# Preparing operands beside a matmul stream: a ring of seven buffers, sums in one engine's order, six steps a pair, and weight preparation spread over steps

## The chip, the cores and the metric

One core of a Trainium2 chip. The metric is the time of one execution on the device in microseconds (us), lower is better. TensorE (PE) multiplies; VectorE (DVE), ScalarE (ACT) and GpSimd (POOL) do the elementwise work; every DMA is issued from SyncE's queue (SP), one after the other.

## What is computed

An attention with packed queries, then two MLPs over its 4608 tokens, cut from the reference:

```python
p_packed = sm_attn(p, k, v)            # 8 batches, 8 heads, 576 tokens, 32 packed queries
x = sm_attn(q, p_packed, p_packed)     # -> 4608 tokens x 512
h = np.maximum(x @ moe_w_in, 0.0)      # first MLP, 2048 wide, squared relu
y = h * h @ moe_w_out
h = y @ moe2_w_in                      # second MLP, 1024 wide
solu = h * softmax(h)
out = (layernorm(solu) * g_ln) @ moe2_w_out
```

All tensors are float32. A product in full precision is made of three fast passes: each operand is split into a rounded part `hi` and a rest `lo`, and `hi*hi + hi*lo + lo*hi` is summed in PSUM. A split costs a cast on ACT (`hi`) and a subtraction on DVE or POOL (`lo`).

## The kernel before

**The stream of steps.** After the first attention stage the kernel runs 256 steps in program order, one per (batch, half of its 576 tokens, chunk of 128 of the 2048 columns), 32 steps per batch. Step i counts from `T0`, so `clock[0]` is `T0 + i`. In a step, `h1` makes six matmuls of 288 columns from a `slot` (attention output folded with `w_in`, loaded from the scratch tensor `pw_d`), ACT takes the relu, POOL squares it (line 420, `gg`; in the first twenty steps ACT does), ACT squares it again as the rounded part (line 421), DVE subtracts (the `split_lo` on line 422, whose instruction is on line 56), and three steps later `ymm` adds twelve matmuls into four PSUM tiles `Y`. After 16 steps `Y` is copied out by ACT and DVE (lines 445 and 447) and the result `y` goes to the scratch tensor `y_d`.

**Side work on the same steps.** `at_step(i, fn)` hangs a job on step i. `load_slot(b, s)` stands 13 steps ahead of the step that reads the slot; for batch 4 the slots wait for the last products `pw`, and slot 7 of it is loaded in step 138 and read in step 142. Three things run in steps 129 to 230:

- `pre_y(m)` (line 690) turns 256 tokens of `y` into the seven operands of a Strassen product for the second MLP, for 14 pairs m. It loads `yf` (one buffer) in its first step i0; `operands` then makes four sums (`comb`, line 668) and seven splits (`split`, casts on line 675, subtractions on line 676), in the steps i0+2 to i0+6; each operand lies in a `yo` tile from a ring of five and is stored to `yc_d` three steps after it was made. The first pair starts at step `R0` = 129 and the next one every `RD` = 7 steps.
- `wi_unit` and `wx_unit` decode the weights of the second MLP, one piece every five steps from step 138 on (`Decode`: a load `raw`, one ACT and three DVE instructions). The last piece of a group calls `quads` (line 585): seven casts on ACT (line 591), seven subtractions (line 592) and four sums (line 587) on DVE, all in one step; its seven stores to `wi_d` or `wx_d` are issued in the step after. There are two such groups for `w_in2` and four for `w_out2`.
- The attention jobs of batches 5 to 7 and the slots' loads.

**What sets the order.** All DMAs are pinned to program order on SP: one that has to wait holds up all that are behind it. The casts of `pre_y`, its sums and subtractions, and the casts of `quads` are pinned too; the rest is placed in each engine's queue by a planner at build time, and each queue runs in that order. After step 230 the pools of the side work are closed, and the weights and first operands of the second MLP are fetched (`load_wi`, `fetch_y`); `h2(0)`, its first product, stands in step 249.

Of the kernel before, what the change touches and what calls it, by code (L numbers as in the profile page):

```python
# [12 lines left out]
F32R = mybir.dt.float32r  # L13
# [9 lines left out]
P = 128  # L23
# [9 lines left out]
def f(ap):  # L33
    return ap.bitcast(F32)


def build(tc, qT, kT, vP, pT, w_in, w_out, w_in2, w_out2, g_ln, out):
# [3 lines left out]
    V, A, G, PE, SP = nc.vector, nc.scalar, nc.gpsimd, nc.tensor, nc.sync  # L41


    pin = tc.keep_in_program_order

    def mm(*a, **k):
        pin(PE.matmul(*a, **k))  # L47
# [4 lines left out]
    def dma(out, in_):  # L52
        pin(SP.dma_start(out=out, in_=in_))

    def split_lo(eng, lo, x, hi):
        eng.tensor_tensor(out=lo, in0=x, in1=f(hi), op=ALU.subtract)  # L56
# [16 lines left out]
    def bank(name):  # L73
        return ps.tile([P, 512], F32, tag="a", name=name, bufs=4)
# [26 lines left out]
    def t25(k, name, dt=F32):  # L101
        return mp.tile([P, KC * P], dt, tag="e" + k, name=name, bufs=2 if k == "1" else 4)
# [157 lines left out]
    T0 = 10  # L260
    ring, clock = [0], [0]
# [141 lines left out]
    def h1(n):  # L403
        b, half, fc = n
        c = slice(half * HF, (half + 1) * HF)
        pb = bank("h1")
        w = slot[b, fc // 2][:, :, fc % 2]
        i = 0
        for g in range(2):
            ah, al = at[b, g]  # L410
            for l, x in ((0, ah), (1, ah), (0, al)):
                mm(pb[:, :HF], w[:, g, l], x[:, c], start=(i == 0), stop=(i == 5))
                i += 1
        rg, g2 = t25("1", "rg"), t25("2", "ghl", F32R)
        r, gg, gh, gl = rg[:, :HF], rg[:, HF:S], g2[:, :HF], g2[:, HF:S]
        A.activation(r, pb[:, :HF], AF.Relu)  # L416
        if clock[0] < T0 + 20:
            A.activation(gg, r, AF.Square)
        else:
            G.tensor_tensor(out=gg, in0=r, in1=r, op=ALU.mult)  # L420
        A.activation(gh, r, AF.Square)  # L421
        split_lo(V, gl, gg, gh)
        gt[n] = (gh, gl)
# [44 lines left out]
    def at_step(i, fn):  # L468
        jobs.setdefault(i if i == "first" else T0 + i, []).append(fn)
# [30 lines left out]
    for b in range(2, B):  # L500
        base = (b - 1) * 32
        js = [s2_jobs(b, g) for g in range(2)]
# [3 lines left out]
        js = [j for x in zip(*js) for j in x]  # L506
# [25 lines left out]
    W2 = {}  # L532
# [30 lines left out]
    def wi_unit(k, q):  # L563
        r0, c0 = (k + 2 * (q // 2)) * P, (q % 2) * 1024

        def fin(wf):
            wq[q] = wf[:, 0]
            if q == 3:
                quads(wi_d[k], 512, *(wq[i] for i in range(4)))

        return Decode(W2["d"], w_in2[r0:r0 + P, c0:c0 + 1024], (1, 512), fin, bufs=(3, 1, 6))

    def wx_unit(k, half):
        q = k + 4 * half

        def fin(wf):
            A.activation(wf[:, 0], wf[:, 0], AF.Copy, scale=W2["g"][:, q:q + 1])
            for i in range(2):
                wq[2 * half + i] = wf[:, 0, i * 256:(i + 1) * 256]
            if half:  # L580
                quads(wx_d[k], 256, *(wq[i] for i in range(4)))

        return Decode(W2["d"], w_out2[q * P:(q + 1) * P], (1, 512), fin, bufs=(3, 1, 6))

    def quads(dst, n, b11, b12, b21, b22):
        def sub(out, x, y):
            V.tensor_tensor(out=out, in0=x, in1=y, op=ALU.subtract)

        def split(o, x):
            t = W2["d"].tile([P, 1024], F32R, tag="op", name="op", bufs=5)  # L590
            pin(A.copy(t[:, :n], x))
            V.tensor_tensor(out=t[:, n:2 * n], in0=x, in1=f(t[:, :n]), op=ALU.subtract)
            later.append(lambda: dma(dst[WO.index(o)], f(t[:, :2 * n])))

        split("11", b11)
        sub(b11, b12, b11)
        split("T1", b11)
        sub(b12, b22, b12)
        split("22", b22)
        sub(b22, b22, b11)  # L600
        split("21", b21)
        sub(b21, b21, b22)
        split("T3", b12)
        split("T2", b22)
        split("T4", b21)

    X = {}

# [34 lines left out]
    for u in range(16):  # L643
        mk = (lambda u=u: wi_unit(u // 4, u % 4)) if u < 8 else (lambda u=u: wx_unit((u - 8) // 2, u % 2))
        decode_at(p1 + 1 + PD * u, mk)
    t0 = 230
# [12 lines left out]
    def halves(t):  # L659
        return [t[:, x * 256:(x + 1) * 256].rearrange("p (a c) -> p a c", a=2) for x in range(2)]  # L660


    def operands(q, put, eng, keep=lambda x: x):
        a11, a12, a21, a22 = q["11"], q["12"], q["21"], q["22"]

        def comb(out, x, y, op=ALU.subtract):
            e = next(eng)
            return lambda: keep(e.tensor_tensor(out=out, in0=x, in1=y, op=op))

        def split(n, x):  # L670
            e = next(eng)

            def go():
                hi, lo, done = put(n)
                keep(A.copy(hi, x))  # L675
                keep(e.tensor_tensor(out=lo, in0=x, in1=f(hi), op=ALU.subtract))  # L676
                done()
            return go

        return [split("11", a11), comb(a21, a21, a22, ALU.add), split("12", a12), comb(a11, a21, a11),  # L680
                split("S2", a11), split("S1", a21), comb(a12, a12, a11), split("22", a22), comb(a22, a22, a11),
                split("S3", a22), split("S4", a12)]

    def quadrants(yl, yr):
        return {"11": yl[:, :, :P], "12": yr[:, :, :P], "21": yl[:, :, P:], "22": yr[:, :, P:]}


    R0, RD = 129, 7

    def pre_y(m):  # L690
        i0 = R0 + RD * m
        st = {}

        def load():
            t = X["y"].tile([P, 4, 256], F32, tag="yf", name="yf", bufs=1)
            dma(t, y_d[:, :, m * 256:(m + 1) * 256])
            q = quadrants(t[:, :2], t[:, 2:])
            st["ops"] = operands(q, put, cycle([V if x == "V" else G for x in "GGGVVGGGVVG"]), pin)

        def put(n):  # L700
            t = X["y"].tile([P, 512], F32R, tag="yo", name="yo", bufs=5)
            hi, lo = halves(t)

            def done():
                k = clock[0] - T0 + 3
                at_step(k, lambda: dma(yc_d[m][:, AO.index(n)], f(t)))
            return hi, lo, done

        at_step(i0, load)
        for k, js in enumerate(((0, 1), (2, 3), (4, 5), (6, 7, 8), (9, 10))):  # L710
            for j in js:
                at_step(i0 + 2 + k, lambda j=j: st["ops"][j]())

# [4 lines left out]
    for m in range(NPRE):  # L718
        pre_y(m)
# [144 lines left out]
    for t in range(max(max(j for j in jobs if j != "first"), T0 + N + LAG - 1) + 2):  # L864
# [46 lines left out]
        if 0 <= i < N:  # L911
            h1(steps[i])
# [132 lines left out]
```

## Time and profile before

| | before |
|---|---|
| median of three runs | 1254.68 us (1254.35 to 1255.73) |
| profiled execution | 1259.44 us, of which its span is 1257.7 us |
| mean granted TensorE clock | 0.966 |
| busy share: PE, DVE, ACT, POOL | 92%, 70%, 52%, 48% |

The profiled execution is one execution with the recorder on. Busy shares are averages over stages with different limits, so they are read by stretch. The rows below carry the engine, the line of the kernel, the operation, its output and inputs, and in square brackets or after an arrow what the engine waited for.

### The profile page before, as it was taken

Reading aid. Unit: us, or ns where it says so; the run is one execution under the profiler, and the core shown is the slowest. Engines: PE = TensorE matmul, PEld = TensorE weight load, DVE = VectorE, ACT = ScalarE, POOL = GpSimd, SP = SyncE. Lnnn points to the kernel's source line nnn. Section 1 sums busy time; section 2 is a strip of 40 time slices with the busy share of each in tenths; the row PEclk is TensorE's granted clock in tenths of the full one; section 3 lists DMA queues with packets and bytes.
Section 4 is the critical chain, followed back from the end, with each engine's and each line's share of the span. In section 5 each row is a group of like instructions: output and inputs, shape, how many; then the busy total and the mean of one; then the engine's idle time right before and its main releaser. Section 6 shows DMA issues by size and latency. Waiting matters only on the chain. (4 is left out here: it accounts for less than half of the span.)

```text
span 1257.7 us, 23688 instructions
## 1 busy us (share of the span) xinstructions
PE 1157.3 (92%) x8556; PEld 1067.1 (85%) x8556; DVE 875.8 (70%) x1716; ACT 654.8 (52%) x1447; POOL 599.0 (48%) x624
## 2 busy tenths in 40 slices
PE   6568899999999999798997898899989999999998
PEld 3357899898999988797897898889988899989897
DVE  4867588745318658458668565245998889889887
ACT  3465565344436656445555554334555655654654
POOL 1133254534227447556666454321654746654743
PEclk9888899999999999898999898999999999999999
DMA  9676697574265998787567677986124142133201
GB/s 332 201 219 179 192 300 244 181 244 161 68 227 147 270 300 233 218 282 280 201 246 269 223 253 262 346 335 227 39 79 145 38 145 82 58 124 101 85 22 47
DMA packets 125541, 239.06 MB, mean 190 GB/s; under 512 B 16880, under 2 KB 44528, under 8 KB 125424
## 3 DMA queue, kind: packets, MB, share of 16 engines
q1 hardware_dynamic: 125424, 237.55, 57.1%
q8 instruction: 67, 1.10, 0.3%
q14 instruction: 50, 0.41, 0.1%
HBM read 144.71 MB, written 91.75 MB: 188 GB/s over the span
## 5 line engine op out<-in xcount | busy, mean ns | idle before, releaser
L47 PE MATMUL Y<-ghl,woh 128*128 128x288 f32 x2048 | 476.1, 308 | 12.5 <-ACT ys L445 6.0
L47 PEld LDWEIGHTS Y<-ghl,woh 128*128 128x128 f32 x2048 | 355.7, 195 | 28.2 <-ACT ys L445 7.4
L420 POOL TENSOR_TENSOR rg<-rg 128x288 f32<-128x288 f32 x236 | 182.5, 776 | 269.0 <-ACT rg L416 243.0
L47 PE MATMUL Y<-ghl,wol 128*128 128x288 f32 x1024 | 309.9, 303 | 0.0
L47 PE MATMUL h<-ah,slot 128*128 128x288 f32 x1024 | 218.8, 302 | 47.3 <-DMA slot<-pw_d 27.1
L56 DVE TENSOR_TENSOR ghl<-rg,ghl 128x288 fp32r<-128x288 f32 x256 | 148.2, 585 | 144.0 <-POOL rg L420 108.5
L47 PEld LDWEIGHTS h<-ah,slot 128*128 128x128 f32 x1024 | 169.4, 194 | 51.5 <-DMA slot<-pw_d 24.2
L47 PEld LDWEIGHTS Y<-ghl,wol 128*128 128x128 f32 x1024 | 199.8, 195 | 0.0
L949 POOL TENSOR_TENSOR cl<-raw,ch 128x512 fp32r<-128x512 f32 x100 | 144.5, 1464 | 108.5 <-ACT ch L948 53.2
L416 ACT ACTIVATE rg<-h 128x288 f32<-128x288 f32 x256 | 104.7, 409 | 175.5 <-PE h L47 154.5
L770 PE MATMUL o<-wx,ch 128*128 128x256 f32 x1008 | 190.8, 287 | 4.9 <-DVE ys L787 2.5
L770 PEld LDWEIGHTS o<-wx,ch 128*128 128x128 f32 x1008 | 160.2, 192 | 11.6 <-DVE ys L787 3.4
L47 PE MATMUL h<-al,slot 128*128 128x288 f32 x512 | 153.3, 299 | 0.0
L770 PE MATMUL o<-wx,cl 128*128 128x256 f32 x504 | 142.4, 286 | 0.4 <-POOL cl L949 0.4
L421 ACT ACTIVATE ghl<-rg 128x288 fp32r<-128x288 f32 x256 | 113.7, 444 | 23.9 <-PE Y L47 18.4
L948 ACT CAST ch<-raw 128x512 fp32r<-128x512 f32 x126 | 76.7, 621 | 62.9 <-DVE raw L954 55.8
L47 PEld LDWEIGHTS h<-al,slot 128*128 128x128 f32 x512 | 98.7, 193 | 0.4 <-POOL al L56 0.4
L770 PEld LDWEIGHTS o<-wx,cl 128*128 128x128 f32 x504 | 95.9, 191 | 2.2 <-POOL cl L949 0.6
L56 POOL TENSOR_TENSOR ws<-dw,ws 128x512 fp32r<-128x512 f32 x32 | 42.3, 1322 | 92.1 <-ACT ws L273 77.3
L770 PE MATMUL h<-wi,y 128*128 128x512 f32 x312 | 83.7, 403 | 0.0
L954 DVE TENSOR_TENSOR raw<-raw 128x512 f32<-128x512 f32 x70 | 76.9, 1110 | 6.1 <-ACT raw L964 4.5
L676 POOL TENSOR_TENSOR yo<-yf,yo 128x256 fp32r<-128x256 f32 x70 | 58.0, 834 | 40.6 <-ACT yo L675 35.8
(144 smaller groups left out, 1869.2 us busy)
## 6 DMA issues: line engine op xcount, KB each, us to landing
pw_d<-pws SPq DMA_DIRECT2D x124, 256.0 KB, 4.5
slot<-pw_d SPq DMA_DIRECT2D x62, 512.0 KB, 6.2
yc_d<-yo SPq DMA_DIRECT2D x98, 256.0 KB, 5.2
y<-yc_d SPq DMA_DIRECT2D x92, 256.0 KB, 4.4
raw<-w_in SPq DMA_DIRECT2D x40, 512.0 KB, 6.6
raw<-w_out SPq DMA_DIRECT2D x24, 512.0 KB, 6.2
kf<-kT SPq DMA_DIRECT2D x32, 288.0 KB, 5.9
out<-ys SPq DMA_DIRECT2D x72, 128.0 KB, 1.7
```

What stands on the lines that cost most here:

```text
L47: pin(PE.matmul(*a, **k))
L56: eng.tensor_tensor(out=lo, in0=x, in1=f(hi), op=ALU.subtract)
L416: A.activation(r, pb[:, :HF], AF.Relu)
L420: G.tensor_tensor(out=gg, in0=r, in1=r, op=ALU.mult)
L421: A.activation(gh, r, AF.Square)
L676: keep(e.tensor_tensor(out=lo, in0=x, in1=f(hi), op=ALU.subtract))
L770: PE.matmul(bk, x, w[:, y], start=(i == 0), stop=(i == 3 * nk - 1))
L948: A.copy(c[n][0], x)
L949: eng.tensor_tensor(out=c[n][1], in0=x, in1=f(c[n][0]), op=ALU.subtract)
L954: eng.tensor_tensor(out=out, in0=x, in1=y, op=op)
```

## The change

Five edits. (1) `pre_y` starts at step 138 instead of 129 and takes six steps a pair instead of seven; its eleven operations stand on four steps (2, 2, 3, 4) instead of five (2, 2, 2, 3, 2). (2) The ring `yo` has seven buffers instead of five. (3) All four sums `comb` and five of seven subtractions are on POOL, two subtractions (operands 12 and 22) on DVE; before, POOL had two sums and five subtractions, DVE two and two. (4) `quads` does three of its jobs in its own step and the rest in the three steps after it, three, three and two at a time. (5) The decodes have two `raw` buffers instead of three, and in every other step from 138 to 229 the square `gg` is made by ACT instead of POOL.

```diff
-        if clock[0] < T0 + 20:
+        if clock[0] < T0 + 20 or T0 + R0 <= clock[0] < T0 + t0 and clock[0] % 2:
             A.activation(gg, r, AF.Square)
         else:
             G.tensor_tensor(out=gg, in0=r, in1=r, op=ALU.mult)
...
-        return Decode(W2["d"], w_in2[r0:r0 + P, c0:c0 + 1024], (1, 512), fin, bufs=(3, 1, 6))
+        return Decode(W2["d"], w_in2[r0:r0 + P, c0:c0 + 1024], (1, 512), fin, bufs=(2, 1, 6))
...
-        return Decode(W2["d"], w_out2[q * P:(q + 1) * P], (1, 512), fin, bufs=(3, 1, 6))
+        return Decode(W2["d"], w_out2[q * P:(q + 1) * P], (1, 512), fin, bufs=(2, 1, 6))
...
-        split("11", b11)
-        sub(b11, b12, b11)
-        split("T1", b11)
-        sub(b12, b22, b12)
-        split("22", b22)
-        sub(b22, b22, b11)
-        split("21", b21)
-        sub(b21, b21, b22)
-        split("T3", b12)
-        split("T2", b22)
-        split("T4", b21)
+        for k, js in enumerate((((split, "11", b11), (sub, b11, b12, b11), (split, "T1", b11)),
+                                ((sub, b12, b22, b12), (split, "22", b22), (sub, b22, b22, b11)),
+                                ((split, "21", b21), (sub, b21, b21, b22), (split, "T3", b12)),
+                                ((split, "T2", b22), (split, "T4", b21)))):
+            for fn, *x in js:
+                if k:
+                    at_step(clock[0] - T0 + k, lambda fn=fn, x=x: fn(*x))
+                else:
+                    fn(*x)
...
-    R0, RD = 129, 7
+    R0, RD = 138, 6
...
-            st["ops"] = operands(q, put, cycle([V if x == "V" else G for x in "GGGVVGGGVVG"]), pin)
+            st["ops"] = operands(q, put, cycle([V if x == "V" else G for x in "GGVGGGGVGGG"]), pin)
...
-            t = X["y"].tile([P, 512], F32R, tag="yo", name="yo", bufs=5)
+            t = X["y"].tile([P, 512], F32R, tag="yo", name="yo", bufs=7)
...
-        for k, js in enumerate(((0, 1), (2, 3), (4, 5), (6, 7, 8), (9, 10))):
+        for k, js in enumerate(((0, 1), (2, 3), (4, 5, 6), (7, 8, 9, 10))):
```

## Rows read from the trace of the kernel before

**Rows 1.** Busy time in one stretch: us, PE, PEld, DVE, ACT, POOL, PEclk, DMA, GB/s
```profile
505.00:800.00 295.00, 260.12 (x1799) 252.13 (x1798) 186.83 (x306) 149.93 (x379) 172.12 (x208) 0.94 0.74 255
```
**Rows 2.** PE's waits in 505 to 800: total us, times, longest
```profile
PE h L47 <- DMA slot<-pw_d: 22.5, 7, 6.9
PE Y L47 <- ACT ys L445: 5.7, 2, 3.5
PE s L47 <- DMA qf<-qT: 3.6, 1, 3.6
PE Y L47 <- DVE ys L447: 2.7, 4, 0.8
```
**Rows 3.** PE in order of time: start, us, [idle before, releaser]
```profile
518.56 0.85 PE L47 MATMUL h<-ah,slot 128*128 128x288 f32 x2 [6.94 <-DMA slot<-pw_d]
...
577.10 0.61 PE L47 MATMUL Y<-ghl,woh 128*128 128x288 f32 x1 [3.50 <-ACT ys L445]
```
**Rows 4.** ACT in order of time, one relu per step
```profile
802.49 0.41 ACT L416 ACTIVATE rg<-h 128x288 f32<-128x288 f32 x1 [1.52 <-PE h L47]
...
812.12 0.41 ACT L416 ACTIVATE rg<-h 128x288 f32<-128x288 f32 x1 [1.52 <-PE h L47]
```
**Rows 5.** Waits of SP's queue in 505 to 800: total us, times, longest
```profile
SPq L53 <- DVE yo L676: 74.0, 14, 11.7
SPq L53 <- DVE op L592: 42.3, 21, 6.5
```
**Rows 6.** SP's queue in order of time: start, us until the last is issued
```profile
503.91 2.86 SPq L53 DMA_DIRECT2D pw_d<-pws  x4
506.87 1.16 SPq L53 DMA_DIRECT2D yf<-y_d  x1
...
512.50 0.43 SPq L53 DMA_DIRECT2D slot<-pw_d  x1
...
572.44 13.30 SPq L53 DMA_DIRECT2D wi_d<-op  x7
...
601.26 0.52 SPq L53 DMA_DIRECT2D yf<-y_d  x1
...
615.80 0.52 SPq L53 DMA_DIRECT2D yf<-y_d  x1
...
768.55 7.70 SPq L53 DMA_DIRECT2D wx_d<-op  x7
...
782.36 0.52 SPq L53 DMA_DIRECT2D yf<-y_d  x1
```
**Rows 7.** DMA issues on the page: count, KB each, us from issue to landing
```profile
pw_d<-pws SPq DMA_DIRECT2D x124, 256.0 KB, 4.5
slot<-pw_d SPq DMA_DIRECT2D x62, 512.0 KB, 6.2
...
yf<-y_d SPq DMA_DIRECT2D x14, 512.0 KB, 4.4
```
**Rows 8.** ACT's wait ahead of the casts of pre_y, 500 to 800
```profile
ACT yo L675 <- DMA yc_d<-yo: 35.9, 22, 7.3
```
**Rows 9.** Groups by line in 505 to 800: count, busy us, mean ns, idle before
```profile
L420 POOL TENSOR_TENSOR rg<-rg 128x288 f32<-128x288 f32 x100 | 82.7, 831 | 77.4 <-ACT rg L416 75.8 <-DMA wx_d<-op 1.0
...
L676 POOL TENSOR_TENSOR yo<-yf,yo 128x256 fp32r<-128x256 f32 x66 | 54.7, 835 | 40.2 <-ACT yo L675 35.6 <-DMA yc_d<-yo 4.6
L421 ACT ACTIVATE ghl<-rg 128x288 fp32r<-128x288 f32 x99 | 44.0, 444 | 2.2
...
L668 POOL TENSOR_TENSOR yf<-yf 128x256 f32<-128x256 f32 x26 | 22.1, 852 | 1.4 <-DVE yf L668 1.3
L668 DVE TENSOR_TENSOR yf<-yf 128x256 f32<-128x256 f32 x26 | 22.0, 848 | 27.0 <-POOL yf L668 23.2 <-POOL yo L676 3.8
...
L676 DVE TENSOR_TENSOR yo<-yf,yo 128x256 fp32r<-128x256 f32 x26 | 14.3, 548 | 11.6 <-ACT yo L675 11.3
...
L47 PE MATMUL s<-qf,slc 128*64 128x288 f32 x32 | 5.7, 487 | 3.6 <-DMA qf<-qT 3.6
```

## The prediction

> **What bounds the kernel now.** I read four views: busy time by stretch, the waits of PE, the queue of SP in order of time, and the groups by line. The change touches steps 129 to 230, so only the stretch from 505 to 800 us counts, which holds nearly all of them. Just behind it nothing disturbs the stream: four steps go by in 812.12 - 802.49 = 9.63 us, 2.41 us a step [rows 4]. That is PE's own pace.
>
> Between 505 and 800 us the pace is worse. PE stands idle for 22.5 + 5.7 + 3.6 + 2.7 = 34.5 us [rows 2], and its mean clock is 0.94 [rows 1]; 0.06 of 295 us is 17.7 us more, since the granted clock falls from its 2.4 GHz level towards 1.2 GHz after each stop. Together **52 us** are lost here. This is all that the change can win.
>
> No engine is full: DVE is busy for 187, POOL for 172 and ACT for 150 of 295 us [rows 1]. What ends the waits is mostly a DMA, the load of a slot [rows 2]. A slot is asked for 13 steps ahead, 13 x 2.41 = 31.3 us, and lands 6.2 us after its issue [rows 7]. So SP can be about 25 us behind PE before a slot comes late. SP is behind because it waits in order: 74.0 us in front of subtractions of `pre_y` on DVE, 42.3 us in front of those of `quads` [rows 5]. A load of `yf`, which has one buffer, cannot be issued until the last operation of the pair before has read it, and stores of operands cannot be issued before their subtraction is done; slots stand behind both.
>
> I therefore count in **pairs**: the interval from one load of `yf` to the next is the period of the side work. From 506.87 to 782.36 there are twelve intervals [rows 6]: 275.5 us, 23.0 us a pair, where seven steps at PE's pace are 16.9 us. An interval in which SP meets no group of `quads` stores is 615.80 - 601.26 = 14.5 us [rows 6]; it includes the load's landing, 4.4 us [rows 7]. That is the period that the pair itself needs when it is behind and nothing stops it. There are six groups of `quads` stores; the first holds SP for 13.30 us, the last for 7.70 [rows 6], and all six for 60.9 us. So 275.5 = 12 x 14.5 (174) + 60.9 + **40.6 of all else** (ring, decodes, other loads).
>
> Does this account give the loss that is there? PE needs 84 steps x 2.41 = 202 us for the same twelve pairs, and 5.7 us for the attention's score matmuls [rows 9]. The side work needs 275.5, so it falls some 68 us behind; 25 of that is free, 43 becomes stops and slow clock. With the batch-4 slot (6.94 us of idle [rows 3] and about 2 us at the slower clock) that is 52. It fits, so I use the same account for the change.
>
> **Part by part.**
>
> *Later start, six steps.* The stores and the load ahead of the batch-4 slot leave its way. That slot was issued at 512.50; ahead of it in the queue stood the first load and stores of pairs that now start at step 138 [rows 6]. Its data leave with the `pw_d` stores from 503.91, which land 4.5 us after issue [rows 7], so it could go at about 509, 3.5 us sooner: 6.94 becomes about 3.4, with the clock 4.5 of the 9 us remain. In return 13 intervals have to fit into 78 steps, 78 x 2.41 + 5.7 = 194 us, 14.9 us each. Six steps a pair alone makes nothing faster: the side work gets less time, and this edit by itself would add to the lag.
>
> *The order of the sums.* Per pair two sums go from DVE to POOL (852 ns there, 848 ns on DVE [rows 9]) and the subtractions stay at five and two. Over 14 pairs DVE loses 28 x 0.848 = 23.7 us and POOL gains 23.9 us. The chain on POOL is then four sums and five subtractions, 4 x 0.852 + 5 x 0.835 = 7.6 us, three casts that stand in the way (up to 0.44 us each, as an ACT instruction on 288 columns [rows 9]) and the squares between them, one or two of 0.83 us: about 10.2 us, and with the landing of the load 14.6 us. Before, DVE stood idle for 27.0 us in front of its two sums [rows 9], the price of handing them between the engines; that goes, but POOL has more to do itself. I keep 14.5 us per pair, with bounds of 13.5 (half of that idle, 1 us a pair, falls off the chain) and 16.2 (both moved sums, 1.7 us, lie on it in full).
>
> The Trainium skill speaks against this part: by "GPSIMD Engine Reference", section 4.1, elementwise work with two inputs is about twice as slow on POOL and belongs on DVE. Here the sums take the same on both [rows 9] and only the subtractions differ, 835 to 548 ns, a factor of 1.5. By the rule the two moved sums would cost 1.7 us each on POOL and the pair 16.2 us or more, an estimate from that page's factor; the trace does not bear it out for the sums.
>
> *Squares on ACT.* 46 squares leave POOL, 46 x 0.831 = 38.2 us, and come to ACT at 0.444 us (the second square beside them [rows 9]), 20.4 us. With the sums POOL goes from 172 to 158 us and DVE from 187 to 163, ACT from 150 to 170, in a stretch of some 250 us: none is full. I cost this at nothing by itself; it is cover for the fuller POOL. If ACT's relu came late by it, PE would wait for ACT in `h1`; no such wait is there now [rows 2], and the three steps between `h1` and `ymm` hide up to 7 us.
>
> *The ring of seven.* With five buffers for seven operands a pair, a cast waits for a store that landed five operands ago. ACT waits 35.9 us ahead of these casts [rows 8]; part of it is the landing of `yf`, which the row does not separate. The waits that do not follow a load of `yf` are about half, 17 us. I take those out of the 40.6 us of all else; bounds 0 and 36. In 13 intervals the rest is 40.6 x 13/12 - 17 = 27 us.
>
> *Quads over four steps.* Eleven DVE and seven ACT instructions are the same in number; what changes is that SP meets two or one stores a step instead of seven, and that the copies of `Y` and the two DVE subtractions of a pair stand behind three instructions instead of eleven. The waits of `ymm` for the copies, 5.7 + 2.7 us [rows 2], stand mostly at such a group (the 3.50 us at 577.10 [rows 3] lies in the group of 572.44 [rows 6]). No trace shows the spread form. Its bounds are 0 (every store is ready when SP comes) and 60.9 us (the planner packs them together again, or SP merely waits four times). I take 24 us, about 4 a group, since SP can still wait once in each of the four steps for the two or three instructions that DVE has to do more in it, at about 1 us each time.
>
> *Two buffers for `raw`.* A piece is read four steps after its load and the buffer is asked for again ten steps after it: six steps, 14 us, of cover. Nothing, unless DVE falls behind by more; then SP waits there and the slots behind it too. From 0 to 5 us.
>
> **The sum.** 13 x 14.5 (188.5) + 24 + 27 = 240 us of side work against 194 us of PE: 46 behind, 25 of them free, 21 lost, and 4.5 at the batch-4 slot: 25.5 us instead of 52. The gain is 26.5 us. The profiled execution would go from 1259.4 to about 1233 us. It stood 4.8 us above the median of the runs, which I take to stay: 1254.7 - 26.5 = 1228.2, or **1229 us** with a little for D below.
>
> **The rivals.** *A, all the lag goes.* If the spread costs nothing and the ring takes 36 us, the sum is 188.5 + 8 = 197 us, 3 behind, and only the batch-4 slot is left: a gain of 47, 1207 us. For it: no engine is full. Against it: DVE and ACT each wait for others in order, and half of "all else" has no name. 14%.
>
> *B, the pair does not fit into six steps: slower.* POOL carries the whole chain, `yf` still has one buffer, and every pair loads behind the last subtraction of the one before. It decides at the interval between loads: the loss is again 52 when the side work is 194 + 25 + 47.5 = 266.5 us, 20.5 us a pair. Above that the change is slower by 13 us for each us of interval. With 16.2 us a pair, 45 us of quads and 27 of the rest it is 283 us, 21.7 a pair, 16 us slower: 1271 us. For it: the present interval is 23.0 and the start is nine steps later with the same end. Against it: 14.5 us has been reached, and the moved squares make room on POOL. 17%.
>
> *C, the spread changes little.* The DVE parts of `quads` are not pinned and the planner places them where it likes; SP waits as long as before for the last of them, while the ring's 17 us and the copies' waits are won. 188.5 + 45 + 27 = 260 us, a gain of 6, 1249 us; at 51 us of quads it is nothing. 21%: 13% for a gain above 2.5 us and 8% for no change.
>
> *D, given back at the second MLP.* `h2(0)` in step 249 needs weights whose loads SP begins in step 231; if PE stops less before that while SP is still 25 us behind, PE waits there instead. At most about 6 us of the gain; I hold it within the forecast's own range, 1215 to 1243 us.
>
> **How the numbers follow.** Forecast 48%, A 14%, B 17%, C 21%. A measurement of this kernel tells some 0.2%, 2.5 us, from no change. Faster: 48 + 14 + 13 = 75%; same 8%; slower 17%. The range goes from A's time to beyond C, a third of the way into B: 1206 to 1262 us. About 5% lie below it and 11% above.
>
> **What the profile after would show.** Right: loads of `yf` some 18 us apart (13 intervals in 240 us), PE's wait for slots down from 22.5 to under 12 us, SP's wait for `quads` down to about half or less, no long ACT wait for `yc_d` except behind a load of `yf`, the batch-4 slot issued by 510 us, mean clock from 505 on above 0.96. Wrong: intervals above 20 us or a POOL that waits for DVE's two subtractions in every pair (B), the seven stores of a group still some 10 us from first to last with SP waiting (C), or a new PE wait in `h2(0)` for weights above 6 us (D).

## The result, and the profile after

| | before | changed |
|---|---|---|
| median of four runs | 1254.86 us (1254.35 to 1255.73) | 1237.86 us (1234.55 to 1243.27) |
| profiled execution, span | 1259.44 us, 1257.7 us | 1236.75 us, 1235.0 us |
| ratio | | 0.9868 (95%: 0.9831 to 0.9905) |

The change makes the kernel 1.3% faster, 16.6 us on 1255. Forecast were 26 us and 1229 us, within 1206 to 1262. The two profiled executions lie further apart than the medians, 22.7 us: that of the kernel before was 4.6 us above its median, that of the changed kernel 1.1 us below. The lines below are read beside those of the kernel before. `pre_y`'s sums and subtractions have moved up by two lines (666 and 674 for 668 and 676, casts 673 for 675).

**Where the gain lies.** DVE in order of time, its first copy of `Y` after a run of 16 steps, just ahead of the changed steps and at three later places (before, then changed):

```profile
479.94 0.45 DVE L447 COPY ys<-Y 128x288 f32<-128x288 f32 x1
...
531.51 0.46 DVE L447 COPY ys<-Y 128x288 f32<-128x288 f32 x1 [1.60 <-PE Y L47]
...
666.34 0.45 DVE L447 COPY ys<-Y 128x288 f32<-128x288 f32 x1
...
812.91 0.46 DVE L447 COPY ys<-Y 128x288 f32<-128x288 f32 x1 [1.56 <-PE Y L47]
```
```profile
477.09 0.45 DVE L447 COPY ys<-Y 128x288 f32<-128x288 f32 x1
...
523.04 0.45 DVE L447 COPY ys<-Y 128x288 f32<-128x288 f32 x1
...
654.37 0.46 DVE L447 COPY ys<-Y 128x288 f32<-128x288 f32 x1 [0.24 <-PE Y L47]
...
790.02 0.46 DVE L447 COPY ys<-Y 128x288 f32<-128x288 f32 x1 [1.60 <-PE Y L47]
```

At the first of these the changed kernel is already 2.9 us ahead, before the changed steps begin; at the next it is 8.5, then 12.0 and at the last 22.9. So 20.0 of the 22.7 us between the two profiled executions are won in the steps that the change touches, and nothing is given back in the second MLP.

**What PE waits for now.** Busy time in the stretch (us, PE, PEld, DVE, ACT, POOL, PEclk, DMA, GB/s) and PE's waits in it; 785 us in the changed kernel is about as far in the steps as 800 us was:

```profile
505.00:785.00 280.00, 258.67 (x1837) 251.41 (x1837) 174.74 (x282) 165.44 (x435) 164.49 (x198) 0.96 0.78 279
...
PE Y L47 <- ACT ys L445: 13.2, 5, 4.6
PE h L47 <- DMA slot<-pw_d: 4.0, 1, 4.0
PE Y L47 <- DVE ys L447: 2.1, 3, 1.0
PE Y L47 <- DVE ghl L56: 1.8, 3, 1.1
```

The waits for slots fell from 22.5 us to 4.0, the wait for `qf` is gone [rows 2], and the mean clock rose from 0.94 [rows 1] to 0.96. Idle plus slow clock is 21.1 + 0.04 x 280 = 32 us instead of 52, the same 20 us. But the waits for copies of `Y` have grown, from 8.4 us [rows 2] to 15.3.

**The side work.** SP in order of time: the `pw_d` stores for the last slots of batch 4, the slot, then the first and the last load of `yf` (start, us):

```profile
496.51 2.85 SPq L53 DMA_DIRECT2D pw_d<-pws  x4
502.89 0.40 SPq L53 DMA_DIRECT2D gl_sb<-g_ln  x1
503.34 0.57 SPq L53 DMA_DIRECT2D slot<-pw_d  x1
...
504.43 0.58 SPq L53 DMA_DIRECT2D yf<-y_d  x1
...
750.10 0.53 SPq L53 DMA_DIRECT2D yf<-y_d  x1
```

The thirteen intervals take 750.10 - 504.43 = 245.7 us, 18.9 a pair instead of 23.0. The batch-4 slot leaves at 503.34 instead of 512.50 [rows 6], and the 6.94 us stop that it caused [rows 3] is gone. ACT's waits ahead of the casts of `pre_y`, and SP's:

```profile
ACT yo L673 <- DMA yf<-y_d: 21.7, 10, 6.0
ACT yo L673 <- POOL yf L666: 17.7, 14, 3.0
...
ACT yo L673 <- DMA yc_d<-yo: 5.5, 5, 3.5
```
```profile
SPq L53 <- POOL yo L674: 73.2, 14, 9.5
SPq L53 <- DVE op L592: 49.8, 22, 6.9
```

The wait for a ring buffer has shrunk from 35.9 us [rows 8] (part of which was the landing of `yf`) to 5.5. What is left is the landing of `yf` itself. SP waits for `quads` no less than before (42.3 us [rows 5]).

### The profile page after: what moved, and what is told of

It reads as the page before. It is cut to its first block, busy times and chain, and to the rows that moved or that the text cites. A ratio compares the mean times of both kernels' runs of the same rounds, so it can differ in the third digit from the quotient of the medians.

```text
span 1235.0 us, 23639 instructions
## 1 busy us (share of the span) xinstructions
PE 1147.7 (93%) x8556; PEld 1057.7 (86%) x8556; DVE 858.2 (69%) x1688; ACT 665.4 (54%) x1493; POOL 585.5 (47%) x606
## 5 line engine op out<-in xcount | busy, mean ns | idle before, releaser
L47 PE MATMUL Y<-ghl,woh 128*128 128x288 f32 x2048 | 470.8, 305 | 20.5 <-ACT ys L445 13.7
L47 PEld LDWEIGHTS Y<-ghl,woh 128*128 128x128 f32 x2048 | 349.7, 192 | 36.9 <-ACT ys L445 15.8
L47 PE MATMUL Y<-ghl,wol 128*128 128x288 f32 x1024 | 306.5, 299 | 0.0
L420 POOL TENSOR_TENSOR rg<-rg 128x288 f32<-128x288 f32 x190 | 142.6, 751 | 213.8 <-ACT rg L416 199.6
L47 PEld LDWEIGHTS Y<-ghl,wol 128*128 128x128 f32 x1024 | 196.8, 192 | 0.0
L47 PEld LDWEIGHTS h<-ah,slot 128*128 128x128 f32 x1024 | 168.0, 192 | 32.8 <-issue 13.5
L421 ACT ACTIVATE ghl<-rg 128x288 fp32r<-128x288 f32 x256 | 113.2, 442 | 21.7 <-PE Y L47 17.4
```

## The experiments

Twelve kernels, each timed against the kernel before on its chip. The column "us" is the ratio's distance from 1, times 1255 us; "loads" are the first and last load of `yf` in the profiled execution, thirteen intervals apart, and "sum" is the time between them. The last two rows are variants of the kernel before, with twelve intervals between the loads shown; the kernel before takes 275.5 us for these.

| kernel | median us | ratio, 95% | us | loads | sum |
|---|---|---|---|---|---|
| changed | 1237.86 | 0.9868, 0.9831 to 0.9905 | -16.6 | 504.43, 750.10 | 245.7 |
| quads in one step | 1250.04 | 0.9952, 0.9936 to 0.9968 | -6.0 | 507.11, 760.35 | 253.2 |
| squares on POOL | 1248.08 | 0.9933, 0.9911 to 0.9954 | -8.4 | 507.80, 761.03 | 253.2 |
| old engine order | 1231.29 | 0.9805, 0.9773 to 0.9838 | -24.5 | 508.64, 747.25 | 238.6 |
| all three undone | 1253.13 | 0.9951, 0.9932 to 0.9971 | -6.1 | 506.44, 764.35 | 257.9 |
| ring of six | 1266.62 | 1.0067, 1.0046 to 1.0088 | +8.4 | 505.55, 773.65 | 268.1 |
| copies of `Y` on DVE | 1239.15 | 0.9842, 0.9824 to 0.9860 | -19.8 | 506.83, 754.10 | 247.3 |
| four `op` buffers | 1242.55 | 0.9876, 0.9850 to 0.9901 | -15.6 | 510.03, 758.72 | 248.7 |
| two `yf` buffers | 1220.87 | 0.9698, 0.9680 to 0.9716 | -37.9 | 506.89, 728.06 | 221.2 |
| two `yf`, old order | 1217.93 | 0.9685, 0.9658 to 0.9711 | -39.5 | 504.39, 727.76 | 223.4 |
| the same, all squares on ACT | 1215.65 | 0.9666, 0.9638 to 0.9693 | -41.9 | 506.32, 722.15 | 215.8 |
| before, quads spread | 1256.92 | 1.0009, 0.9990 to 1.0028 | +1.1 | 507.04, 776.29 | 269.3 (twelve) |
| before, squares on ACT | 1246.69 | 0.9899, 0.9883 to 0.9915 | -12.7 | 505.20, 766.23 | 261.0 (twelve) |

**Quads in one step again.** The loop of four groups is replaced by the straight list.

```diff
-        for k, js in enumerate((((split, "11", b11), (sub, b11, b12, b11), (split, "T1", b11)),
...
-                    fn(*x)
+        split("11", b11)
+        sub(b11, b12, b11)
...
+        split("T4", b21)
```

> The changed kernel with all eleven jobs of quads in one step again. The account of the prediction (PE loses what the side work takes beyond PE's own time and 25 us) puts 37 us on this part: loads of yf about 21.5 us apart instead of 18.9, and 1255 to 1265 us. Rival: spreading moved nothing, because SP's wait for quads did not fall in the changed kernel (42.3 us before, 49.8 after): within 4 us of the changed kernel, 1234 to 1242 us.

Measured: 1250.04 us, between the two: the spread is worth 10.6 us, not 17 to 27 and not nothing. The intervals grew by 0.6 us, not 2.6. The difference lies in PE's waits for slots, 20.4 us instead of 4.0, while its waits for copies of `Y` are shorter, 7.7 us instead of 15.3. SP in order of time shows how (this kernel, then the changed one, the first group of `w_in2` in both):

```profile
563.78 13.74 SPq L53 DMA_DIRECT2D wi_d<-op  x7
577.62 1.23 SPq L53 DMA_DIRECT2D slot<-pw_d  x2
```
```profile
561.73 2.45 SPq L53 DMA_DIRECT2D wi_d<-op  x2
564.27 0.81 SPq L53 DMA_DIRECT2D slot<-pw_d  x1
565.88 5.64 SPq L53 DMA_DIRECT2D wi_d<-op  x3
571.61 0.42 SPq L53 DMA_DIRECT2D slot<-pw_d  x1
...
577.92 2.49 SPq L53 DMA_DIRECT2D wi_d<-op  x2
```

From first to last the seven stores take longer in the spread form, 18.7 us instead of 13.7, but slots go out between them, the first 13 us sooner. Behind a later group of the packed form PE stops for 11.29 us; the slot that it misses was issued behind the group and behind a load of `yf`:

```profile
731.79 9.19 SPq L53 DMA_DIRECT2D wx_d<-op  x7
...
745.84 0.52 SPq L53 DMA_DIRECT2D yf<-y_d  x1
...
747.74 0.66 SPq L53 DMA_DIRECT2D slot<-pw_d  x1
```
```profile
753.56 0.85 PE L47 MATMUL h<-ah,slot 128*128 128x288 f32 x2 [11.29 <-DMA slot<-pw_d]
```

The stop is not the group's alone: from 725 to 755 us SP waits 5.4 us for `quads` and 8.7 us for POOL's subtractions of `pre_y`.

**Old engine order.**

```diff
-            st["ops"] = operands(q, put, cycle([V if x == "V" else G for x in "GGVGGGGVGGG"]), pin)
+            st["ops"] = operands(q, put, cycle([V if x == "V" else G for x in "GGGVVGGGVVG"]), pin)
```

> The changed kernel with the sums of a pair shared between DVE and POOL as before (two sums each, five and two subtractions). The prediction kept 14.5 us a pair for both orders: within 5 us of the changed kernel, 1233 to 1243 us. Rival: the hand-overs between the two engines are what made a pair long (DVE idle 27.0 us before its two sums): loads of yf 1 us or more further apart, 13 us slower, 1245 to 1255 us.

Measured: 1231.29 us, faster than the changed kernel by some 7 us; the intervals of the two ratios overlap at their edge, so its size is uncertain. The loads are 0.5 us closer together. Neither theory expected this sign: sums in one engine's order do not pay here.

**Squares on POOL again.**

```diff
-        if clock[0] < T0 + 20 or T0 + R0 <= clock[0] < T0 + t0 and clock[0] % 2:
+        if clock[0] < T0 + 20:
```

> The changed kernel with every square gg on POOL again. The prediction costed the move at nothing: 1234 to 1242 us. Rival: POOL's queue is what paces a pair, and the two or three squares of 0.8 us that come back into it lengthen each pair by 1.5 to 2.5 us: 1250 to 1270 us.

Measured: 1248.08 us, 8.2 us slower than with the squares on ACT; my "nothing" fell. ACT's waits for POOL's sums in this kernel (below) are nearly twice the 17.7 us above, and its waits for `yf` and the ring have grown too, though ACT itself has less to do:

```profile
ACT yo L673 <- POOL yf L666: 33.3, 20, 4.1
ACT yo L673 <- DMA yf<-y_d: 27.2, 10, 6.0
...
ACT yo L673 <- DMA yc_d<-yo: 12.0, 9, 5.0
```

**Before, with quads spread.** The new loop in the kernel before, nothing else (the diff of the first experiment, reversed).

> The kernel before with quads spread over four steps and nothing else. The account of the prediction: 37 us less side work, of 43 us lost: 1225 to 1235 us. Rival: spreading by itself moves nothing, or costs, as SP has to wait in four steps instead of one: 1250 to 1262 us.

Measured: 1256.92 us, no difference. The rival held. The spread pays only together with the rest of the change; PE's wait for slots stays at 19.6 us there (22.5 before [rows 2]). Its twelve intervals are 6.2 us shorter than those of the kernel before, and the time did not follow.

**Six steps and the ring alone.** The changed kernel with the three edits above undone at once.

> The changed kernel with the engine order, the squares and quads as before: what is left is the later start, six steps a pair, the ring of seven and two buffers for raw. The account of the prediction says side work 13 x 14.5 + 61 + 27 = 277 us against 194 us of PE, 62 us lost instead of 52: 1260 to 1270 us. Rival, from the four runs so far (squares worth 10, quads worth 12 in the changed kernel, the new order minus 7): the parts add up and the rest is worth 2 us: 1250 to 1256 us. Second rival: the parts overlap and the rest is worth most of the gain: 1236 to 1246 us.

Measured: 1253.13 us, -6.1 us. The first rival held: undone from the changed kernel, the parts add up. Undone one at a time, quads cost 10.6 us, squares 8.2, and the old order wins 7.9, together 10.9; with these 6.1 it makes 17.0, and 16.6 were measured. My own account, 1260 to 1270 us, fell. From the other side they do not add up: put into the kernel before, the spread is worth nothing.

**Before, with squares on ACT.**

```diff
-        if clock[0] < T0 + 20:
+        if clock[0] < T0 + 20 or T0 + R0 <= clock[0] < T0 + t0 and clock[0] % 2:
             A.activation(gg, r, AF.Square)
```

> The kernel before with every other square from step 129 to 229 on ACT and nothing else. If the squares pay because DVE, which waits in order for POOL's square ahead of the subtraction, is held less, the gain is there without the rest: 1242 to 1250 us. If they pay only where POOL has the longer chain of the changed kernel: within 3 us of before, 1252 to 1258 us.

Measured: 1246.69 us, -12.7 us from this one line (here it acts from step 129 on). The gain does not need the longer chain on POOL. DVE's waits in this kernel, from 500 to 790 us:

```profile
DVE ghl L56 <- POOL rg L420: 29.9, 23, 2.4
...
DVE ghl L56 <- ACT ghl L421: 21.9, 14, 7.9
```

Its wait for POOL's square was 40.6 us in the same stretch of the kernel before, so 11 us of it are gone, while a wait for ACT has come in its place, 21.9 us where it was 1.5. Together the two have grown from 42.1 to 51.8 us: the reason in my expectation, a DVE that is held less, is not what pays, though its time came true. The twelve intervals are 14.5 us shorter. What pays is not shown by this run.

**Ring of six.**

```diff
-            t = X["y"].tile([P, 512], F32R, tag="yo", name="yo", bufs=7)
+            t = X["y"].tile([P, 512], F32R, tag="yo", name="yo", bufs=6)
```

> The changed kernel with six yo buffers instead of seven. If ring waits were the 17 us that the prediction took out, a ring that is one short of a pair brings about half of them back, loads of yf 0.6 us further apart and 6 to 10 us slower, 1243 to 1250 us. If the ring is no longer a limit once it spans nearly a pair: 1234 to 1242 us.

Measured: 1266.62 us, slower than before and 25 us slower than with seven. Both expectations fell short. ACT's waits ahead of the casts in this kernel, from 505 to 800 us:

```profile
ACT yo L673 <- DMA yc_d<-yo: 49.1, 26, 5.7
ACT yo L673 <- POOL yf L666: 20.4, 14, 3.2
```

The wait for a buffer is 49.1 us instead of 5.5, and PE's wait for slots 17.1. The pairs come 1.7 us further apart. Here six steps a pair need the seventh buffer to be faster than the kernel before. Neither this rhythm with five buffers nor a ring of seven with seven steps a pair was run.

**Copies of `Y` on DVE.**

```diff
-                elif oc % 2 == 0 or clock[0] < T0 + 20:
+                elif clock[0] < T0 + R0 and oc % 2 == 0 or clock[0] < T0 + 20:
                     A.copy(o, Y[oc])
```

> The changed kernel with all four copies of Y on DVE from step 138 on. PE waits 13.2 us for copies on ACT, which stand behind casts that wait for yf. If ACT's place behind these casts is what holds the copies: that wait and its slow clock go, 1220 to 1232 us. If DVE is as late at the same points: the wait goes to DVE, 1234 to 1246 us.

Measured: 1239.15 us, not told apart from the changed kernel. PE now waits 11.7 us in eight places for the copies on DVE, instead of 13.2 for those on ACT. The wait goes to whichever engine makes the copies.

**Two `yf` buffers.** The room comes from the `op` ring.

```diff
-            t = X["y"].tile([P, 4, 256], F32, tag="yf", name="yf", bufs=1)
+            t = X["y"].tile([P, 4, 256], F32, tag="yf", name="yf", bufs=2)
...
-            t = W2["d"].tile([P, 1024], F32R, tag="op", name="op", bufs=5)
+            t = W2["d"].tile([P, 1024], F32R, tag="op", name="op", bufs=4)
```

> The changed kernel with two yf buffers, and four op buffers instead of five to make room. If the period of a pair is the chain through the one yf buffer (load waits for the last operation, casts wait for the load), SP's wait ahead of the loads (73 us for POOL) and ACT's wait for yf (22 us) go, and the slots and most copies are in time: 1215 to 1230 us. If the elementwise queues set the period, the waits only move: 1234 to 1242 us.

Measured: 1220.87 us, 21 us faster than the changed kernel, as the first theory said. SP's waits and PE's in this kernel, from 505 to 785 us:

```profile
SPq L53 <- DVE op L592: 63.4, 28, 5.7
SPq L53 <- POOL yo L674: 28.8, 19, 7.2
...
PE Y L47 <- ACT ys L445: 6.3, 3, 2.6
PE Y L47 <- DVE ys L447: 2.2, 3, 0.9
PE Y L47 <- DVE ghl L56: 1.7, 1, 1.7
```

SP's wait for POOL's subtractions, which stood ahead of the load, fell from 73.2 to 28.8 us, the pairs come 17.0 us apart, PE waits for no slot, and the waits for copies fall to 8.5 us. SP's wait for `quads` even rises to 63.4 us, and PE still waits for no slot.

**Four `op` buffers, one `yf`** (the control: only the second line of that diff).

> The changed kernel with four op buffers instead of five and one yf buffer as it has: the control for the run with two yf buffers. If that run's gain came from the second yf buffer: 1234 to 1244 us here. If a part came from the shorter op ring (SP meets the stores of quads differently): below 1230 us.

Measured: 1242.55 us, 0.9876: as the changed kernel. The gain is that of the second `yf` buffer.

**Two `yf` buffers and the old engine order.** Both diffs together.

> The changed kernel with two yf buffers, four op buffers and the engine order of before. If the old order pays by shortening the chain through the one yf buffer (7 us faster with one), the gain is gone with two: 1217 to 1224 us. If it pays because POOL is relieved of two sums a pair: 1211 to 1217 us.

Measured: 1217.93 us, 0.9685 beside 0.9698, not told apart. The median lies in the first range, the one for an order that matters only while one buffer makes the chain; this fits but does not prove it, since the advantage with one buffer was itself at the edge of what can be told.

**The same with all squares on ACT.**

```diff
-        if clock[0] < T0 + 20 or T0 + R0 <= clock[0] < T0 + t0 and clock[0] % 2:
+        if clock[0] < T0 + 20 or T0 + R0 <= clock[0] < T0 + t0:
```

> As the run before, with every square gg from step 138 to 229 on ACT. If DVE's wait for POOL's square (57 us with two yf buffers) is what still holds the stream: 1205 to 1214 us. If ACT becomes the late engine (20 us more on it, copies of Y behind it): 1218 to 1232 us.

Measured: 1215.65 us, the fastest of all: 0.9666, 42 us below the kernel before and some 25 us below the change. The step from the run ahead is within the intervals and outside both expectations, so the other 46 squares neither hurt nor clearly help.

## Why the prediction was right, and where it was off

**The bound: right.** PE's losses were slots that came late and the slow clock behind each stop. They fell from 52 to 32 us, and the time with them.

**The total: right, with luck in it.** In the account's own terms later start, six steps and the ring were to cost 10 us together (62 us lost instead of 52), quads to win 37, squares and order nothing: 26.5 us. Measured, by undoing them, were 6.1 us won, 10.6 won, 8.2 won and 7.9 lost: 17.0. The parts are off by 16, 26, 8 and 8 us. That these errors cancel to 10 us is luck.

**The account in pairs: right in its slope, too generous by 9 us.** The forecast summed to 240 us of side work in thirteen intervals; 245.7 were measured. For the eleven kernels of the table with thirteen intervals, "loss = sum - 194 - 25", never below zero, can be held against the time. For the changed kernel it gives 245.7 - 219 = 27 us lost, a gain of 25 where 16.6 was measured; for two `yf` buffers 2 us lost, a gain of 50 (37.9 measured); for the ring of six 49 lost, a gain of 3 (8.4 slower measured). The gain comes out 4 to 12 us too large, 8.8 on average, over a span of 50 us. For the changed kernel some 6 of the 9 us lie in the executions that were profiled, 4.6 us above the median and 1.1 us below; profile against profile the gain is 22.7 us. What else the account left out is not shown.

That sum and time move together does not show that the period sets the time. The loads stand on the same steps as PE's work, and with two `yf` buffers, where PE waits for no slot, sum and time still agree; in the kernel before, the spread `quads` shortened the sum and not the time. The direction is shown by the two runs that change one ring of the side work alone: the second `yf` buffer wins 22 us against its control, and one `yo` buffer less costs 25.

The 14.5 us that a pair was said to need was the shortest case. Six of the twelve intervals of the kernel before hold no group of `quads` stores. Two of them take 14.5 us; the three from 506.87 [rows 6] over the first three loads below take 20.3, 19.1 and 22.9, and the one from 615.80 [rows 6] to the last load below 21.9:

```profile
527.14 0.57 SPq L53 DMA_DIRECT2D yf<-y_d  x1
...
546.25 0.53 SPq L53 DMA_DIRECT2D yf<-y_d  x1
...
569.12 0.53 SPq L53 DMA_DIRECT2D yf<-y_d  x1
...
637.66 0.52 SPq L53 DMA_DIRECT2D yf<-y_d  x1
```

The account put what they take beyond 14.5 us into "all else".

**Later start, six steps and the ring: wrong in sign.** I held that six steps by themselves would add to the lag, and the account put them, with the ring, at 1260 to 1270 us. They won 6.1 us. Six steps without a longer ring were not run. The batch-4 slot is one reason: I put 4.5 us of its 9 as remaining, and the stop is gone. Its `pw_d` stores, which I had left where they were, leave at 496.51 instead of 503.91 [rows 6]. The other is that the side work took 257.9 us in that run, not the 277 of the account.

**The ring: priced by the wrong number.** I took 17 us for it, at most 36, from what ACT waited in the old rhythm. In the new one a single buffer less costs 25 us, as ACT's wait grows by 43.6 us and the thirteen intervals by 22.4. What the step from five to seven is worth by itself no run isolates.

**Quads: right in sign, wrong in mechanism.** 37 us of relief was forecast, and SP's wait for the group was to halve. It did not (49.8 us), and the spread is worth 10.6 us. The step that failed is the sum of the six stretches, 60.9 us, as the price: here a wait of SP cost time only where a load behind it came late. Spreading let the slots through between the stores; with two `yf` buffers SP waits longer for `quads`, 63.4 us, and no slot is late.

**Squares on ACT: the worst-sized term.** "Nothing by itself", because no engine is full. It is worth 8.2 us in the changed kernel and 12.7 in the kernel before, with POOL busy for 58% of the stretch before [rows 1]. Why is not shown. In the changed kernel ACT's waits for POOL's sums fell with the move, from 33.3 us to 17.7, which fits a POOL whose queue is in order and holds others up; no run tests that alone.

**Order of the sums: no gain, probably a loss of some 7 us.** I kept 14.5 us for both orders, within bounds of 13.5 and 16.2. The loads were 0.5 us further apart with the new order. The hand-overs that I expected to go have moved: before, DVE was idle for 27.0 us ahead of its sums [rows 9]; now POOL's sums wait 14.8 us for DVE's subtractions, a sign that I had named for B. The lines of POOL's sums and subtractions in the changed kernel:

```profile
L666 POOL TENSOR_TENSOR yf<-yf 128x256 f32<-128x256 f32 x56 | 47.5, 848 | 15.2 <-DVE yo L674 14.8
```
```profile
L674 POOL TENSOR_TENSOR yo<-yf,yo 128x256 fp32r<-128x256 f32 x70 | 60.1, 873 | 65.0 <-ACT yo L673 49.7 <-DMA raw<-w_in 6.2 <-DVE ghl L56 5.0
```

POOL was idle for 65.0 us ahead of its subtractions, most of it for ACT's casts; with the old engine order these idle times are 72.7 us, so they do not tell the two orders apart.

By the rule of the Trainium skill ("GPSIMD Engine Reference", section 4.1), elementwise work with two inputs is about twice as slow on POOL and belongs on DVE. The trace agrees in direction for the subtractions: 873 ns on POOL and 630 on DVE here, 835 and 548 before [rows 9]. For the sums the prediction read equal means, 852 and 848 ns. The shortest sums of the kernel before, from 470 to 810 us (min/median/max), come closer to the rule, 717 ns on POOL and 409 on DVE:

```profile
L668 POOL TENSOR_TENSOR yf<-yf x28: 717/787/1185, 483.7 to 790.5; 128x256 f32<-128x256 f32 x28
L668 DVE TENSOR_TENSOR yf<-yf x28: 409/884/1025, 491.6 to 794.2; 128x256 f32<-128x256 f32 x28
```

**Copies of `Y`: wrong.** I expected 8.4 us of waits to go with the packed `quads`; they are 15.3, and 7.7 in the run with packed `quads`. PE has three long waits for copies on ACT, 3.80, 3.05 and 4.58 us. One is plain: the copy stands on ACT behind a cast of `pre_y` that waits for `yf` to land (ACT, then PE):

```profile
527.25 0.40 ACT L673 CAST yo<-yf 128x256 fp32r<-128x256 f32 x1 [3.88 <-DMA yf<-y_d]
527.56 0.39 ACT L445 COPY ys<-Y 128x288 f32<-128x288 f32 x1
```
```profile
528.00 0.61 PE L47 MATMUL Y<-ghl,woh 128*128 128x288 f32 x1 [3.80 <-ACT ys L445]
```

In the other two the copies stand behind several shorter pieces, of the decodes, of `pre_y` and of `quads`, and none of them waits longer than 1.5 us. Moving the copies to DVE did not help. With the second `yf` buffer ACT waits 9.1 us for `yf` instead of 21.7, and the waits for copies fall with it.

**The rivals.** B's decision point, 20.5 us between loads, held closely: the only kernel above it, the ring of six with 20.6, is the only one with six steps that is slower than before. A, all lag gone, comes nearest with the second `yf` buffer: no slot is late, but the time is 1220.87 us, not 1207. C's sign came true and its time did not: SP waits for `quads` as long as before, 49.8 us, but the time is 1237.86 us, not 1249, since slots go out between the stores. D did not happen: PE's longest wait in `h2(0)` is 0.85 us. Two buffers for `raw` are not settled: no run has three beside the ring of seven.

## What to carry to other kernels

Where one in-order DMA queue feeds the main stream and also serves side work, measure the period of the side work, from one load of its smallest ring to the next, before counting busy time: here the two moved together in eleven kernels. Look at the ring with one buffer first, since its load waits for the last reader and the first reader waits for the load; doubling it was worth more here than the whole change. Price a queue's wait by what stands behind it and is late, not by its length, and do not price an instruction on an engine that is not full at zero when others wait in order for it.

## What the runs showed of the hardware that was not expected

DVE's operations on two 128x256 operands scatter by more than a factor of two. The 28 sums above took from 409 to 1025 ns, half of them 884 or more, while ACT's casts on the same data lie between 387 and 415 ns. The mean of DVE's subtractions of `pre_y` was 548 ns before and 630 in the changed kernel, 528 there with the old engine order, but also 666 in the kernel before with squares on ACT, where POOL has less to do. What slows them is not shown.

The four runs of the changed kernel lie 0.7% apart and those of the kernel before in the same comparison 0.1%. This is not the change's doing: beside the experiments the kernel before was timed 8 to 13 times on each of three other chips, and there its own runs lie 0.55 to 0.7% apart.
